# Between the two expert layers of an attention kernel: a row operation ahead of list bookkeeping, two weight loads put behind the last scatter, and weight splits ahead of the transposes

## The chip, the cores and the metric

The program runs on one core of a Trainium2 chip. The time is the device time of one execution in microseconds (us); lower is better. The engines are TensorE (PE in the rows; its weight loads are PEld), VectorE (DVE), ScalarE (ACT), GpSimd (POOL) and SyncE (SP, which only issues transfers here). Transfers run on 16 DMA engines. SP's transfers come from the hardware queue, q1 in the rows; GpSimd's indirect gathers and scatters come from the software queue, q0.

## The reference

Attention with a local window and a few global keys gives `x` (3072 rows of 512). Two layers of experts follow, each row going to one of 8 experts:

```python
x = _moe_ref(x=x, **moe_kwargs)       # layer 1: every row with x @ w_skip > 0 goes to its best expert
return _moe2_ref(x=x, **moe2_kwargs)  # layer 2: experts with a fixed capacity

# layer 2
cap = N // E                          # 384 rows for each expert
logits = x @ w_gate
for idx in np.argsort(-logits.flatten()):   # best (row, expert) pairs first
    tok, e = int(idx) // E, int(idx) % E
    if assigned[tok] >= 0 or counts[e] >= cap:
        continue
    assigned[tok] = e
    counts[e] += 1
for e in range(E):
    mask = assigned == e
    h = np.maximum(x[mask] @ w1[e], 0.0)
    out[mask] = h @ w2[e]
```

Layer 2 needs the finished rows of layer 1, both for its logits and as the input of its experts.

## The kernel before

The kernel is written as streams of work that one planner, a clock of estimated engine times that is kept while the program is built (`Clock`, `ck`), puts into one fixed order for each engine. What is said below of the order is settled at build time.

**Experts.** A unit is one expert's list of rows: up to 208 in layer 1 (blocks of 128 and 80), 384 in layer 2 (three blocks of 128). For a unit, the rows are gathered by an indirect transfer (`gather`, tiles `xg`), turned on TensorE (`pt` or `py` <- `ident,xg`), and kept as a high part `xh` (ScalarE) and a low part `xl` (VectorE). Every weight is split in the same way: `wr` is a loaded part (512 KB; there are eight parts to an expert, four of w1 and four of w2), `wh` its high part (ScalarE), `wl` the rest (`wr` - `wh`), on GpSimd in four pieces or on VectorE in one. `mm1` does 12 products into `ph` for each 128 hidden columns (`xh·wh`, `xl·wh`, `xh·wl`, four of each), then `mm2` 9 into `py`.

**Weights.** The class `Weights` keeps the list of parts (`order`), how many are loaded (`loaded`) and split (`split`). There are four `wr` buffers. `preload` issues loads on SP until four are ahead of the splits; `pump` calls `preload` and then splits a part when its moment has come; `need` splits until a part is there. `on_pool` names the parts whose low half GpSimd makes.

**Routing.** Layer 2's assignment is done in eight phases by the stream of kind `main`. A phase finds one expert's threshold in seven steps over the bits of the logits. A step of phases 0 and 1 is: `gm` (VectorE compares), 24 small matmuls `pr<-oh,gm` that count, `fl` (VectorE), one matmul `pr<-fl,wt`, `v_` and two or three small VectorE operations. After the steps come the bookkeeping (`go`, `part`, `PEN`, `AC`, `rem`, `ML`) and the list of rows (`slots`: `ttb`, `tb_rhs`, `fx`, `mp`, `ix`, `ids`). Phase p's `ids` is what unit p of layer 2 gathers by.

**The place of the change.** `hook` is called ahead of each product and lets a waiting stream put its next step first, if its operands are ready by the planner's clock. At the end of layer 1 `mm2_block` does the last expert's products block by block; after the second block (80 rows) `row_late` makes the rows `o` on VectorE and scatters them into `x2d` on GpSimd. Phase 0 of the routing runs beside these products. Then layer 2 starts: `split_next` makes weight splits of its first expert, `units2[0].load()` gathers its rows (from `x2d`, so after the last scatter has landed), `wait_for` runs the streams and lets TensorE do filler products (`warm`: `ph<-ones,tri`) while it waits, and `run_units` starts the products.

```python
            W_.pump()                      # mm2_block, end of each of the eight steps f
        ...
        W_.add((lambda r0, n: w21r[bass.ds(ereg * Dm + r0, n)], ...))   # phase: this expert's parts
        W_.preload()                       # four loads, as soon as the expert is known
        ...
    split_next()
    units2[0].load()
    split_next()
    split_next()
    wait_for(lambda: units2[0].tb == NH, True)   # gathers, transposes, xh and xl of the three blocks
    split_next()
```

Of the kernel before, what the change touches and what calls it, by code (L numbers as in the profile page):

```python
# [163 lines left out]
def tile_attn_moe_moe(ctx: ExitStack, tc: tile.TileContext, q, k, v, n_global, n_local,  # L164
                      w_skip, w_gate, w1, w2, w2_gate, w21, w22, out):
    nc = Chip(tc.nc)
# [9 lines left out]
    E, _, F = w1.shape  # L176
    KC = Dm // 128
    FC = F // 128
# [6 lines left out]
    HI = -(-SLOTS // 128)  # L185
# [256 lines left out]
    class Weights:  # L442
# [29 lines left out]
            t = max(ck.at["pool"], ck.at["pe"] + T_W) + (4 - j) * 2.3  # L472
            return u == self.done + 1 and j < 4 and t > ck.at["pe"] + (FC - self.f) * 4.2 + T_H

        def preload(self):
            while self.loaded < len(self.order) and self.loaded < self.split + 4:
                self.do_load(self.loaded)

        def pump(self, wait=False):

# [4 lines left out]
                        and (self.pools or (u == 0 and j < 4))):  # L485
                    self.do_split(self.order[self.split])

        def do_load(self, i):
            c = self.order[i]
            u, j = divmod(c, NCH)  # L490
            t = wraw.tile([128, 1024], F32, name="wr")
            a = self.src[u][0 if j < 4 else 1]
            if j < 4:
                nc.sync.dma_start(t, a(j * 128, 128))
            else:
                nc.sync.dma_start(t.rearrange("p (c d) -> p c d", c=2),
                                  a((j - 4) * 256, 256).rearrange("(c p) d -> p c d", p=128))
            self.raw[c] = t
            self.loaded += 1
# [38 lines left out]
    W_ = Weights()  # L538
# [152 lines left out]
    def scatter(dst, ids, src, others):  # L691
        nc.gpsimd.memset(spacer, 0.0)
        st = nc.gpsimd.indirect_dma_start(out=dst, out_offset=bass.IndirectOffsetOnAxis(ap=ids, axis=0),
                                          in_=src, in_offset=None, bounds_check=N - 1, oob_is_err=False)
        for o in others:
            tc.declare_no_dep(st.ins, o.ins, reason="rows of other tokens")
        others.append(st)
# [124 lines left out]
    for g in range(-3, NU + 1):  # L822
# [16 lines left out]
        m, t = divmod(g + 4, NG)  # L839
# [35 lines left out]
    class Unit:  # L875
        at, tb, py, defer, xh, x2, turns, third, banks = None, 0, 0, None, None, None, False, False, None
# [203 lines left out]
    def mm1(U_, f, n_tok):  # L1080
        ph = fps.tile([128, 512], F32, name="ph", bufs=2)
        xx = (U_.xh, U_.xl)
        i = 0
        for (a, b_) in P3:
            for c in range(KC):
                hook(W_.parts[U_.g * NCH + c][a], xx[b_][:, c, :n_tok])
                nc.tensor.matmul(ph[:, :n_tok], W_.parts[U_.g * NCH + c][a][:, f * 128:(f + 1) * 128],
                                 xx[b_][:, c, :n_tok], start=i == 0, stop=i == 3 * KC - 1)
                i += 1
        if U_.defer is None:  # L1090
            h2 = ff.tile([128, 2, wide_h], F32R, name="h2", bufs=h2_bufs)
            hh, hl = h2[:, 0], h2[:, 1]
        else:
            hh, hl = U_.h[0][:, f], U_.h[1][:, f]
            if f == FC // 2 and not U_.defer:
                wait_for(lambda: X_.turned == 2)
        nc.scalar.activation(hh[:, :n_tok], ph[:, :n_tok], AF.Relu)

        def low():
            nc.vector.scalar_tensor_tensor(hl[:, :n_tok], ph[:, :n_tok], 0.0, hh[:, :n_tok].bitcast(F32),  # L1100
                                           op0=OP.max, op1=OP.subtract)

        return (hh, hl) if U_.defer is not None else (hh, hl, h2), low
# [20 lines left out]
    def mm2(U_, f, h, nb, low):  # L1124
        if f == 0:
            U_.y = [fps.tile([128, Dm], F32, name=f"py{(tb + U_.py) % 3}") for tb in range(nb)]
        ww = W_.parts[U_.g * NCH + 4 + f // 2]
        o = (f % 2) * Dm
        for tb in range(nb):
            for i, (a, b_) in enumerate(P3):  # L1130
                hook(h[a], ww[b_])
                n = U_.n[tb]
                nc.tensor.matmul(U_.y[tb][:n], h[a][:, tb * 128:tb * 128 + n], ww[b_][:, o:o + Dm],
                                 start=f == 0 and i == 0, stop=f == FC - 1 and i == 2)
            if tb == 0 and low:
                low()
        W_.free = 4 * U_.g + (f + 1) // 2
# [25 lines left out]
    def need(chunk):  # L1163
        while chunk not in W_.parts:
            b4 = W_.split
            W_.pump(True)
            assert W_.split > b4
# [23 lines left out]
            return max(t, ck.at["dve"] - T_SP) if eng == "dve" else t  # L1191

    streams = []

    def order():
        return sorted((s_ for s_ in streams if not s_.busy), key=lambda s_: s_.rank())

    def hook(*aps):

        while streams:  # L1200
            t = max(ck.at["pe"] + T_EPS, ck.ready("pe", (), aps))
            for s_ in order():
                if s_.when() <= t:
                    s_.step()
                    break
            else:
                return

    def warm(until):

        if ck.at["pe"] + 0.11 <= until:
            p = fps.tile([128, 512], F32, name="ph", bufs=2)
            while ck.at["pe"] + 0.11 <= until:
                nc.tensor.matmul(p[:, :256].rearrange("p (a n) -> p a n", a=2), tri, wide_one, start=True, stop=True)

    def wait_for(over, fill=False):
        while not over():
            t = min(s_.when() for s_ in order()) + T_F
            s_ = next(s_ for s_ in order() if s_.when() <= t)
            if unit_no[0] < 0 and s_.kind == "main":  # L1220
                first_ = min((o for o in order() if o.kind != "main"), key=lambda o: o.when(), default=None)
                if first_ and first_.when() < s_.when() + T_M:
                    s_ = first_
            if fill and s_.need[0] != "dve":
                warm(s_.when() - T_U)
            s_.step()
# [106 lines left out]
    def row_late(U_, tb, on_dve=False):  # L1333
        n = ROWS[tb]
        x2 = ff.tile([128, Dm], F32, name=f"o{tb}", bufs=1)[:n]
        if on_dve:
            nc.vector.scalar_tensor_tensor(x2, U_.y[tb][:n], U_.gw[:n, tb:tb + 1], U_.xs[tb][:n, :Dm],
                                           op0=OP.mult, op1=OP.add)
        else:
            nc.scalar.activation(x2, U_.y[tb][:n], AF.Copy, scale=U_.gw[:n, tb:tb + 1])  # L1340
            nc.gpsimd.tensor_tensor(x2, x2, U_.xs[tb][:n, :Dm], op=OP.add)
        scatter(x2d, U_.sid[:n, tb:tb + 1], x2, x2_st)

    def mm2_block(U_, tb):
        n = ROWS[tb]
        y = U_.y[tb] = fps.tile([128, Dm], F32, name=f"py{(tb + U_.py) % 3}")
        for f in range(FC):
            need(U_.g * NCH + 4 + f // 2)
            ww = W_.parts[U_.g * NCH + 4 + f // 2]
            o = (f % 2) * Dm  # L1350
            for i, (a, b_) in enumerate(P3):
                hook(U_.h[a][:, f], ww[b_])
                nc.tensor.matmul(y[:n], U_.h[a][:, f, tb * 128:tb * 128 + n], ww[b_][:, o:o + Dm],
                                 start=f == 0 and i == 0, stop=f == FC - 1 and i == 2)
            if tb == HI - 1:
                W_.free = 4 * U_.g + (f + 1) // 2
            W_.pump()
# [319 lines left out]
    def phase(ph_):  # L1677
# [104 lines left out]
        dv.tensor_scalar(ei, fx[:, 0:1], -1.0, float(E), op0=OP.mult, op1=OP.add)  # L1782
        ereg = nc.sync.value_load(ei[0:1, 0:1], min_val=0, max_val=E - 1)
        W_.add((lambda r0, n: w21r[bass.ds(ereg * Dm + r0, n)], lambda r0, n: w22r[bass.ds(ereg * F + r0, n)]))
        W_.preload()
        if last:
            yield "dve", ()
            dv.tensor_scalar(fe_p, PEN, 0.0, None, op0=OP.is_ge)
# [70 lines left out]
    def routing():  # L1859
        yield from table_rows(units1[E - 1])  # L1860
        for p in range(E):
            yield from phase(p)
# [25 lines left out]
    for U_ in units1[NE:]:  # L1888
        U_.py = 2 * U_.defer
        if U_.g == E:  # L1890
            U_.y = {}
            for tb in range(HI):
                mm2_block(U_, tb)
                row_late(U_, tb, tb == HI - 1)
            continue
        for f in range(FC):
            need(U_.g * NCH + 4 + f // 2)
            mm2(U_, f, [t[:, f] for t in U_.h], HI, None)
            W_.pump()
        for tb in range(HI):  # L1900
            row_late(U_, tb)
# [2 lines left out]
    ff = ctx.enter_context(tc.tile_pool(name="ff", bufs=2))  # L1904
    width = wide_h = CAP
    h2_bufs = LASTF + 1
    W_.on_pool = (2, 3)
    out_st = []

    def put(U_, tb, o):  # L1910
# [45 lines left out]
    def split_next():  # L1956
        need(W_.order[W_.split])
# [3 lines left out]
    units2[0].banks = ("pt", "py1", "py2")  # L1961
    units2[0].load()
    ck.late = 2.0
    split_next()
    split_next()
    wait_for(lambda: units2[0].tb == NH, True)
    split_next()
    warm(ck.ready("pe", (), [units2[0].xh]) - T_U)
    W_.on_pool = range(NCH)

# [35 lines left out]
```

## Time and profile before

| | us |
|---|---|
| median of 3 runs | 784.69 (783.55 to 793.27) |
| the profiled execution | 787.59 |
| its span, first to last instruction | 785.8 |
| TensorE busy in it | 752.7 (96%) |
| VectorE busy | 529.5 (67%) |
| ScalarE busy | 403.0 (51%) |
| GpSimd busy | 463.2 (59%) |

The profiled execution took 1.8 us more than its span, and 2.9 us more than the median of the runs. Times in the rows are counted from the span's start: attention lies ahead of 234 us, layer 1 runs from there to 457 us, layer 2 from 476 us to the end. Busy time of TensorE includes the filler products.

### The profile page before, as it was taken

What the parts mean: (1) busy time and instruction counts of PE and PEld (TensorE: products, weight loads), DVE (VectorE), ACT (ScalarE), POOL (GpSimd) and SP (SyncE); (2) the same over time, 40 slices, a digit from 0 to 9 for tenths busy, and PEclk for the clock granted to TensorE, in tenths of its full rate; (3) what the DMA queues carried; (4) which work ended last, traced back from release to release, by engine and by line L of the source; (5) the groups of instructions that cost most, each with busy time, mean ns of one, the idle gap of its engine ahead of it and who ended that gap; (6) DMA issues with size and microseconds to landing.
All of it is one profiled execution on the core that took longest, in us unless ns stands there. A gap on an engine that the chain in (4) does not pass through costs nothing.

```text
span 785.8 us, 17475 instructions
## 1 busy us (share of the span) xinstructions
PE 752.7 (96%) x5942; PEld 635.8 (81%) x5942; DVE 529.5 (67%) x1950; ACT 403.0 (51%) x934; POOL 463.2 (59%) x807
## 2 busy tenths in 40 slices
PE   6999999899889899999989989999999999999997
PEld 5887777777669899999888667888788888798986
DVE  5987988979456766676763586878778778822110
ACT  4887787887546455465652214344343434445221
POOL 3664556754214556557652636787685959599711
PEclk9999999999999999999999999999999999999999
DMA  8686988987616757677670061636263535455210
GB/s 190 161 215 167 248 225 205 242 213 213 201 28 209 246 186 218 227 234 231 213 245 6 19 219 59 202 102 220 97 201 141 179 135 162 147 176 188 79 41 40
DMA packets 143834, 132.23 MB, mean 168 GB/s; under 512 B 65427, under 2 KB 110739, under 8 KB 143744
## 3 DMA queue, kind: packets, MB, share of 16 engines
q1 hardware_dynamic: 135360, 111.19, 48.3%
q0 software_dynamic: 6784, 19.51, 7.2%
q8 instruction: 48, 0.79, 0.4%
q10 hardware_dynamic: 1600, 0.39, 0.2%
q14 instruction: 42, 0.34, 0.1%
HBM read 108.80 MB, written 22.79 MB: 167 GB/s over the span
## 4 chain that ended last, share of the span: by engine, by line
PE 51%; issue 6%; POOL 5%; DVE 4%; DMA 3%; ACT 1%; POOLq 0%; ACTq 0%; DVEq 0%
PE ph L125 23%; PE py L125 22%; PE pr L125 3%; POOL wl L125 3%; PE pt L125 2%; DMA wr<-in_moe_w_dram 2%; DVE wl L125 1%; ACT wh L125 1%; POOL out_dram L125 1%; DMA xg<-x2d,ids 1%; DVE py L125 0%; POOL x2d L125 0%; POOL xt L125 0%; DVE xl L125 0%; DVE o L125 0%
## 5 line engine op out<-in xcount | busy, mean ns | idle before, releaser
L125 POOL TENSOR_TENSOR wl<-wr,wh 128x256 fp32r<-128x256 f32 x340 | 245.7, 755 | 67.0 <-ACT wh L125 66.5
L125 ACT ACTIVATE wh<-wr 128x1024 fp32r<-128x1024 f32 (+1 forms) x148 | 142.0, 985 | 42.1 <-DMA wr<-in_moe_w_dram 22.2
L125 PE MATMUL py<-wh,h 128*128 128x512 f32 (+1 forms) x448 | 158.1, 405 | 0.0
L125 ACT ACTIVATE h<-ph 128x208 fp32r<-128x208 f32 (+2 forms) x132 | 54.5, 415 | 188.9 <-PE ph L125 184.1
L125 POOL TENSOR_SCALAR pb<-pb,st 128x232 f32<-128x232 f32 (+1 forms) x192 | 83.6, 454 | 73.8 <-ACT pb L125 26.3
L125 DVE SCALAR_TENSOR_TENSOR h<-ph,h 128x208 fp32r<-128x208 f32 (+1 forms) x128 | 58.9, 461 | 98.5 <-ACT h L125 98.3
L125 ACT ACTIVATE pb<-sb,st 128x232 f32<-128x232 f32 (+1 forms) x192 | 113.8, 663 | 10.4 <-DVE st L125 9.9
L125 PE MATMUL ph<-xh,wh 128*128 128x208 f32 (+1 forms) x512 | 100.5, 313 | 1.8 <-DVE h L125 1.8
L125 PE MATMUL ph<-xh,wl 128*128 128x208 f32 (+1 forms) x512 | 101.1, 313 | 0.0
L125 PE MATMUL ph<-xl,wh 128*128 128x208 f32 (+1 forms) x512 | 99.4, 313 | 0.0
L125 PEld LDWEIGHTS py<-wh,h 128*128 128x128 f32 (+1 forms) x448 | 81.7, 186 | 14.3
L125 PE MATMUL py<-wl,h 128*128 128x512 f32 (+1 forms) x224 | 90.3, 403 | 0.0
L125 PEld LDWEIGHTS ph<-xh,wh 128*128 128x128 f32 x512 | 83.2, 192 | 7.1 <-DVE h L125 1.9
L125 PEld LDWEIGHTS ph<-xl,wh 128*128 128x128 f32 x512 | 80.0, 193 | 1.4 <-issue 1.0
L125 PEld LDWEIGHTS ph<-xh,wl 128*128 128x128 f32 x512 | 80.2, 193 | 0.2
L125 DVE TENSOR_TENSOR wl<-wr,wh 128x1024 fp32r<-128x1024 f32 x51 | 66.0, 1300 | 18.5 <-ACT wh L125 17.2
L125 DVE CUSTOM_DVE_ANT_0 sb<-pS,bias 128x232 f32<-128x232 f32 (+1 forms) x192 | 61.4, 375 | 8.6 <-PE pS L125 7.2
L125 DVE COPY pts<-pP 116x512 f32<-116x512 f32 (+1 forms) x96 | 60.7, 672 | 7.6 <-PE pP L125 7.1
L125 PE MATMUL pS<-kt,qt 64*128 64x232 f32 (+1 forms) x384 | 50.6, 382 | 1.0 <-ACT pb L125 1.0
L125 POOL DMA_INDIRECT xg<-x2d,ids x24 | 23.2, 968 | 47.6 <-DVE py L125 31.4
L125 PE MATMUL pP<-ident,pb 128*116 128x128 f32 (+1 forms) x384 | 50.7, 275 | 0.0
L125 PE MATMUL pO<-pts,vw 116*64 116x128 f32 x640 | 46.3, 281 | 4.0 <-DVE pts L125 2.6
(461 smaller groups left out, 1276.3 us busy)
## 6 DMA issues: line engine op xcount, KB each, us to landing
wr<-in_moe_w_dram SPq DMA_DIRECT2D x136, 512.0 KB
xd<-xs SPq DMA_DIRECT2D x32, 192.0 KB
x2d<-xs SPq DMA_DIRECT2D x32, 192.0 KB
kraw<-in_k_dram SPq DMA_DIRECT2D x30, 192.0 KB
qraw<-in_q_dram SPq DMA_DIRECT2D x30, 192.0 KB
vw<-in_v_dram SPq DMA_DIRECT2D x32, 160.0 KB
vw<-in_v_dram SPq DMA_DIRECT2D x32, 120.0 KB
xT<-in_moe_w_dram SPq DMA_DIRECT2D x1, 1536.0 KB
```

Source lines behind the costliest of these rows:

```text
L125: r = f(*a, **k)
```

## The change

The edits:

- **A hold on the routing.** From the seventh of the eight steps of the last expert's second block on, `hook` no longer lets the stream `main` put steps that start on VectorE ahead of the products. The hold ends after `row_late`.
- **Two loads instead of four.** Phase 0 preloads two weight parts instead of four. After the hold ends, `preload(4, True)` loads up to four, and writes one element of each buffer on GpSimd ahead of the load (`gate`).
- **One more split on VectorE.** Of the first four parts of layer 2, GpSimd makes the low half of one (number 3) instead of two (2 and 3).
- **Splits ahead of the transposes.** The fourth `split_next` moves ahead of `wait_for`.

```diff
-        def preload(self):
-            while self.loaded < len(self.order) and self.loaded < self.split + 4:
-                self.do_load(self.loaded)
+        def preload(self, ahead=4, gate=False):
+            while self.loaded < len(self.order) and self.loaded < self.split + ahead:
+                self.do_load(self.loaded, gate)
...
+            if gate:
+                nc.gpsimd.memset(t[0:1, 0:1], 0.0)
...
-                if s_.when() <= t:
+                if s_.when() <= t and not (held_back and s_.kind in held_back and s_.need[0] == "dve"):
...
+            if tb == HI - 1 and f == FC - 2:
+                held_back.append("main")
...
-        W_.preload()
+        W_.preload(4 if ph_ else 2)
...
+            held_back.clear()
+            if len(W_.order) > W_.split:
+                W_.preload(4, True)
             continue
...
-    W_.on_pool = (2, 3)
+    W_.on_pool = (3,)
...
-    split_next()
-    split_next()
+    for _ in range(3):
+        split_next()
     wait_for(lambda: units2[0].tb == NH, True)
-    split_next()
```

**VectorE, from the last two list operations ahead of the last expert's rows.** `o` is the row operation; `go`, `part`, `PEN` and `AC` are bookkeeping. Before:

```order
L125 CAST tb_rhs<-py_7053 128x24
L125 TENSOR_TENSOR go<-oh,py_7053 128x192
L125 TENSOR_TENSOR py_7053<-py_7053,fe 128x24
L125 TENSOR_REDUCE part<-go 128x8
L125 TENSOR_TENSOR py_7053<-py_7053,code 128x24
L125 SCALAR_TENSOR_TENSOR PEN<-py_7053,PEN 128x24
L125 TENSOR_TENSOR AC<-AC,py_7053 128x24
L125 SCALAR_TENSOR_TENSOR o_7549<-py_7405,gwt,xg_6495 80x512
L125 COPY fx<-pt 128x1
```

And now:

```order
L125 CAST tb_rhs<-py_7053 128x24
L125 SCALAR_TENSOR_TENSOR o_7541<-py_7405,gwt,xg_6495 80x512
L125 COPY fx<-pt 128x1
L125 TENSOR_TENSOR fx<-fx,py_7053 128x1
L125 TENSOR_SCALAR tb_rhs<-fx 128x1
L125 TENSOR_SCALAR pt<-islot,fx 128x384
L125 TENSOR_TENSOR tb_rhs<-pt,tb_rhs 128x1
L125 SCALAR_TENSOR_TENSOR mp<-islot,fx,pt 128x384
L125 TENSOR_TENSOR go<-oh,py_7053 128x192
```

The row operation and six list operations now stand ahead of six bookkeeping operations. Later on VectorE three splits `wl` follow `ids`, where two did, and `rem` and `ML` stand behind them.

**GpSimd, from the scatter of the last expert's first block.** `x2d<-o` are the scatters, `xg<-x2d` the gathers of layer 2's first expert. In the changed program:

```order
L125 DMA x2d<-o_7398,sid 3072x512
L125 MEMSET spacer 1x1
L125 DMA x2d<-o_7541,sid 3072x512
L125 DMA xg_7604<-x2d,ids 128x512
L125 DMA xg_7606<-x2d,ids 128x512
L125 DMA xg_7608<-x2d,ids 128x512
L125 TENSOR_TENSOR wl<-wr,wh 128x256 x20
```

No write into a `wr` buffer stands between the last scatter and the gathers, nor anywhere else: `pump` at the end of the same step of `mm2_block` has called `preload` with its default of four, so that nothing is left for the gated call. On SP the order of all transfers is the same as before; the four loads of w1 stand behind the read of the expert's number (`ei`) in both:

```order
L120 TENSOR_LOAD ei
L120 ISA x2
L125 ISA
L125 DMA wr<-in_moe_w_dram 128x1024
L125 ISA
L125 DMA wr<-in_moe_w_dram 128x1024
L125 ISA
L125 DMA wr<-in_moe_w_dram 128x1024
L125 ISA
L125 DMA wr<-in_moe_w_dram 128x1024
```

**ScalarE, behind the last rows of layer 1.** `wh` are high parts of weights, `xh` those of the gathered rows. Before:

```order
L125 ACTIVATE wh<-wr 128x1024 x3
L125 ACTIVATE xh<-pt 128x4x128
L125 ACTIVATE xh<-py_7772 128x4x128
L125 ACTIVATE xh<-py_7818 128x4x128
L125 ACTIVATE wh<-wr 128x1024
L125 ACTIVATE h_7961<-ph 128x384
```

And now:

```order
L125 ACTIVATE wh<-wr 128x1024 x4
L125 ACTIVATE xh<-pt 128x4x128
L125 ACTIVATE xh<-py_7751 128x4x128
L125 ACTIVATE xh<-py_7769 128x4x128
L125 ACTIVATE h_7852<-ph 128x384
```

All four high parts are now made ahead of the first `xh`. On TensorE, counted in the order between the last product of layer 1 and the first of layer 2: 72 counting matmuls (three routing steps) before, 24 (one step) now; the other two steps now stand among the products of layer 2's first expert. The fillers there are 106 before and 104 now, 66 of them in one row ahead of the first gathered block now. In the whole program two splits move from GpSimd to VectorE (340 pieces before, 332 now).

## Rows read from the trace of the kernel before

**Rows 1.** Busy time by engine, clock, DMA share in stretches: PE, PEld, DVE, ACT, POOL.

```profile
520.00:560.00 40.00, 40.00 (x253) 32.67 (x251) 31.03 (x136) 15.89 (x24) 32.13 (x48) 1.00 0.43 145
```

**Rows 2.** Timeline of TensorE between the layers: start, us, operation, idle before.

```profile
462.78 4.86 PE L125 MATMUL ph<-ones,tri 128*128 128x256 bf16 x43
...
470.72 0.66 PE L125 MATMUL pt<-ident,xg 128*128 128x128 f32 x4 [1.50 <-DMA xg<-x2d,ids]
...
476.20 0.76 PE L125 MATMUL ph<-xh,wh 128*128 128x384 f32 x3
...
478.38 0.44 PE L125 MATMUL ph<-xl,wh 128*128 128x384 f32 x1
```

**Rows 3.** Timeline of GpSimd: the last scatter and the first gather.

```profile
459.72 0.92 POOL L125 DMA_INDIRECT x2d<-o,sid  x1 [6.82 <-DVE fx L125]
...
466.21 1.00 POOL L125 DMA_INDIRECT xg<-x2d,ids  x1 [5.57 <-DVE py L125]
```

**Rows 4.** Timeline of VectorE from the last product of layer 1.

```profile
457.33 0.17 DVE L125 CAST tb_rhs<-py 128x24 bf16<-128x24 f32 x1
...
458.70 0.74 DVE L125 SCALAR_TENSOR_TENSOR o<-py,gwt,xg 80x512 f32<-80x512 f32 x1
...
462.45 0.16 DVE L125 SCALAR_TENSOR_TENSOR ids<-pt,ix 128x3 int32<-128x3 f32 x1
462.53 1.23 DVE L125 TENSOR_TENSOR wl<-wr,wh 128x1024 fp32r<-128x1024 f32 x1
```

**Rows 5.** DMA queues, 460.7 to 463.0 us: packets, MB, share of 16 engines.

```profile
q1 hardware_dynamic: 220, 0.79, 96.2%
```

**Rows 6.** DMA queues, 463.0 to 465.5 us.

```profile
q1 hardware_dynamic: 109, 0.32, 52.4%
q0 software_dynamic: 64, 0.15, 15.1%
```

**Rows 7.** DMA issues, 444.4 to 446.0 us: the scatter issued there, us to landing.

```profile
x2d<-o,sid POOLq DMA_INDIRECT x1, 2.4
```

**Rows 8.** DMA queues and issues, 383.1 to 386.0 us, in layer 1.

```profile
q1 hardware_dynamic: 303, 1.11, 97.9%
...
xg<-xd,gid POOLq DMA_INDIRECT x1, 5.6
```

**Rows 9.** Timeline of SP: weight loads.

```profile
456.44 2.16 SPq L125 DMA_DIRECT2D wr<-in_moe_w_dram  x4
...
472.58 0.37 SPq L125 DMA_DIRECT2D wr<-in_moe_w_dram  x1
```

**Rows 10.** DMA queues, 467.2 to 468.9 us.

```profile
q1 hardware_dynamic: 219, 0.44, 68.0%
q0 software_dynamic: 1, 0.00, 0.6%
```

**Rows 11.** Chain that ended last, two routing steps beside products in layer 1.

```profile
446.36 0.69 PE pr L125 x24
...
447.81 1.59 PE py L125 x6
449.40 0.69 PE pr L125 x24
```

**Rows 12.** Stretches again: the last products, and the start of layer 1.

```profile
776.00:780.00 4.00, 4.00 (x19) 3.26 (x18) 0.00 (x0) 0.60 (x1) 2.10 (x4) 1.00 0.16 66
234.00:238.00 4.00, 3.92 (x22) 3.46 (x23) 2.01 (x3) 2.87 (x4) 1.70 (x2) 0.57 0.39 110
```

**Rows 13.** Timeline of TensorE at the start of layer 1.

```profile
234.08 1.54 PE L125 MATMUL py<-ident,xg 128*128 128x128 f32 x8 [2.14 <-issue]
```

**Rows 14.** Timeline of GpSimd and TensorE: the second expert's third block.

```profile
501.08 0.95 POOL L125 DMA_INDIRECT xg<-x2d,ids  x1 [0.30 <-issue]
...
513.39 0.60 PE L125 MATMUL pt<-ident,xg 128*128 128x128 f32 x4
```

More of the change, by code (lines that the diff above doesn't have):

```diff
@@ L486, in pump, with do_load @@
                     self.do_split(self.order[self.split])
-        def do_load(self, i):
+        def do_load(self, i, gate=False):
             c = self.order[i]
@@ L1193, in tile_attn_moe_moe @@
     streams = []
+    held_back = []
     def order():
```

## The prediction

> **What bounds the kernel now.** I read the stretches first. From the second expert of layer 2 on TensorE is busy all the time: 40.00 of 40.00 us between 520 and 560 [rows 1]. So whatever moves the first product of layer 2, at 476.20 us [rows 2], moves the end by as much, and whatever is added to TensorE behind it is paid in full. The change touches the road to that product, so I read the timeline there, engine by engine. The reader is to see three things.
>
> First, TensorE has nothing but fillers to do, and at the end nothing at all: it sits idle for 1.50 us until the first gathered block lands at 470.7 [rows 2]. Second, the gather starts only at 466.21, though its list `ids` is ready at 462.6 [rows 3, 4]: it waits for the last scatter, issued at 459.72, to land. Third, the queues say why that takes so long. From 460.7 to 463.0 us all packets are of the hardware queue, the four weight loads issued at 456.44 to 458.60; the scatter's 64 packets move from 463.0 on, when those loads run out [rows 5, 6, 9]. The same scatter without loads beside it lands 2.4 us after its issue [rows 7], here the wait is 6.5 us. In layer 1 a gather issued in the middle of loads fares alike: its queue shows no packet in 383.1 to 386.0, and it lands after 5.6 us [rows 8].
>
> **The change part by part.** The sum is made against the profiled execution (787.59 us), in differences, and laid on the median of the runs, 784.69.
>
> *The row operation first.* The last list operation ahead of it begins at 457.33, so `o` can begin at about 457.5 instead of 458.70 [rows 4]: 1.2 us earlier, and the scatter with it, at 458.5. What is late next is the queue: the fourth load is still issued by 458.60 [rows 9], so the scatter still stands behind all four, whose packets run out at the same time. I take no gain, since the case of rows 8 (issued among the loads, drained behind them) is the nearest; the bounds are 0 and -1.2.
>
> The Trainium skill has another rule: its page "DMA: Bandwidth & Descriptors", section "Queues, rings and completion order", says that each DMA engine takes turns between the queues that have work. By that rule the scatter would not wait for the loads to drain, and the 1.2 us would be had in full. The trace speaks against it: 220 packets of one queue and none of the other in 2.3 us, with the scatter's issue done [rows 3, 5].
>
> *Two loads behind the scatter.* The order shows that this does not happen: the four loads stand in SP's queue as they did, with no write of GpSimd ahead of them. Cost and gain 0, both bounds: the operations are not in the program.
>
> *Bookkeeping behind the list.* `ids` comes about 0.5 us sooner (1.2 for `o` and the six operations moved up, less the 1.3 of bookkeeping, plus the 0.6 of `rem` and `ML`, which move behind it). That list was ready 3.6 us before the gather began [rows 3, 4], so it is worth nothing.
>
> *The third split on VectorE.* It gives its `wr` buffer back when the three splits, one of 1.23 us each [rows 4], are through, at 465.6 to 466.1. GpSimd's version came behind the three gathers and freed it at 472.58, when SP issues that load [rows 9]. So a 512 KB load moves from behind the gathers to right ahead of them. Before, the gathers' packets wait for the one load that runs at 467.2 to 468.9 (219 packets to 1) [rows 10]; now two follow each other. A load needs 1.5 us at 0.79 MB in 2.3 us [rows 5]. The bounds are 0 and +1.5; I take half, **+0.7**, since the load in front is moved up by 0.5 and part of the second falls into the 0.5 us that the gathers need to start anyway (an estimate from the middle of the bounds). The first block lands at 471.4.
>
> *From the landing to the first product.* Before: 470.72 to 476.20, 5.5 us, with two more routing steps put in between. Now the order has 12 transposes (3 times 0.6 to 0.66), 24 counting matmuls (0.69), one `fl` matmul and 15 fillers of 0.113 (4.86 us for 43) [rows 2, 11], 4.5 us in all. VectorE's `xl` and `fl` and ScalarE's `xh` end within that. **-1.0**. Moving the fourth high part ahead of the transposes lies under the wait for the gather and costs nothing: its load has drained by 464 [rows 6].
>
> *Waits among the first products.* Before, three products of 0.18 each from 476.20, one step's count of 0.69 and one more product should end at 477.6; the next starts at 478.38 [rows 2, 11]. These 0.8 us were waits for that step's `gm` and for the last `xl`. Now the fillers stand where the first was, and the third `xl` comes a step earlier against the products. **-0.8**, bounds 0 and -0.8.
>
> *Two routing steps more among the products.* Before, three steps are counted in the time that TensorE waits anyway; now one. All seven phases have to be done, so two steps go to where TensorE is full. What a step costs there: in layer 1 a step and eight products take 3.04 us; at 0.265 a product (1.59 for six) a step is 0.9, at 0.21 (19 in 4.00 us) it is 1.36 [rows 11, 12]. I take 1.15: **+2.3**, bounds +1.8 and +2.7.
>
> *The clock.* Fillers now end before the gather lands: 66 of them at 0.113 from about 460.9 last until 468.3, and then TensorE idles for 2.4 us (landing at 470.7) to 3.1 us (471.4), where it idled for 1.50. At the start of layer 1 it idled for 2.14 us, and behind that the granted clock was 0.57 on the average of 234 to 238 us, so at the lower of the two levels, 1.2 GHz, for most of it [rows 12, 13]; that cost (1 - 0.57) times 4.0, 1.7 us. After the 1.50 us the clock stayed at 2.4 GHz. The longer idle is nearest to the 2.14 us, so I count on a fall. The bounds are 0 and +1.7; part of the slow time may pass while TensorE still waits, so I take **+1.2**.
>
> The sum: 0 + 0.7 - 1.0 - 0.8 + 2.3 + 1.2 = +2.4 us. That makes 787.1 for the median, and a span of 788.2 in a profile like the one before. This is 0.3% slower, well inside the 2% (15.7 us) that a measurement of this kernel can tell from no change.
>
> **The rivals.** *The clock holds.* For it: the fall depends on more than the length of the idle time, and the rows have one case either way. Then +1.2, **785.9**.
>
> *The queues share.* If the scatter, 1.2 us earlier, also lands 1.2 us earlier, the gathers start at 465.0, ahead of the third load; the first block lands near 469.5, the idle time is 1.2 us and the clock holds: -1.2 - 1.0 - 0.8 + 2.3 = -0.7, **784.0**. Against it speak rows 5, 6, 8 and 10. This is where the page's turn-taking would lead.
>
> *The steps are free.* If gaps of TensorE among the first expert's products swallow the two counts, 2.3 us fall away: **784.8**. Against it: TensorE shows no free time beside routing [rows 1].
>
> *The list comes late.* This ends on the slower side. The routing of phase 1 runs two steps later against the products, 3.04 us each at the pace of rows 11, so 6 us. The second expert's third block is gathered from 501.08 (landed some 3.3 us later) and turned at 513.39 [rows 14], a slack of 9 us. If other work delays the stream by three more steps, the lag is 15 us, TensorE waits for 6, and the time is **793**. It decides at a lag of 9 us.
>
> *The change does what it says.* With two loads less ahead of it the scatter would land up to 3 us sooner; the order excludes it.
>
> **How the numbers follow.** Forecast 0.45, clock holds 0.22, queues share 0.17, steps free 0.08, late list 0.05, others 0.03. The range goes from the case of shared queues, less the 1.1 us by which the fastest run lies under the median, 783.0, to the forecast with the upper bounds of load, steps and clock (+0.8 + 0.4 + 0.5, so 788.8) and some of the same spread, 789.5. That leaves out the late list and some of the edges. No case reaches 2% on either side; faster by 2% has 0.01, slower by 2% 0.02 (a late list that repeats in later phases), within 0.97.
>
> **What the profile would show.** The scatter issued near 458.5 but the gathers still beginning near 466 say that the queue decides; a gather at 465.0 or before says that they share. A weight load issued near 466 and a first gathered block after 471 confirm the collision. The clock column between 470 and 476 shows whether it fell. The first product near 476 to 477, and 150 counting matmuls in the first expert instead of 108, show that the gain went into the two steps. A first product before 474 with the end unmoved would still fit the steps; an end moved with it would break that term. The prediction is wrong if the scatter lands early, or if the planner's new order of the later experts differs by more than a microsecond or two.

## The result and the profile after

The changed kernel takes 790.36 us (median of 13 runs, 788.85 to 794.68) where the kernel before takes 786.64 in the runs beside it (13 runs, 783.02 to 793.27). The ratio is 1.0057, with an interval of 1.0041 to 1.0073, so 3.2 to 5.7 us slower. The forecast was 2.4 us slower, 787.1; the direction holds, the time is outside the range. A part of that is the base: the forecast was laid on a median of three runs, 784.69, and the 13 runs of the same kernel here have 786.64.

The two profiled executions ran apart by 3.9 us ahead of the transition already: the `ttb` matmul right behind the last product of layer 1 starts at 457.47 before and at 453.54 after. So all times of the road below are counted from that matmul. TensorE (start, us, operation, idle before), first that matmul in the kernel before, then the changed kernel:

```profile
457.47 0.16 PE L125 MATMUL pt<-ttb,tri 128*128 128x1 bf16 x1
```

```profile
453.54 0.16 PE L125 MATMUL pt<-ttb,tri 128*128 128x1 bf16 x1
...
456.92 7.37 PE L125 MATMUL ph<-ones,tri 128*128 128x256 bf16 x66
467.94 1.09 PE L125 MATMUL pt<-ident,xg 128*128 128x128 f32 x4 [3.66 <-DMA xg<-x2d,ids]
...
474.51 0.95 PE L125 MATMUL ph<-xh,wh 128*128 128x384 f32 x4
...
517.29 0.97 PE L125 MATMUL ph<-xh,wh 128*128 128x384 f32 x4 [0.69 <-ACT xh L125]
...
519.13 0.44 PE L125 MATMUL ph<-xl,wh 128*128 128x384 f32 x1 [0.50 <-DVE xl L125]
```

Against [rows 2] the reader is to see three things: the fillers end early and TensorE idles for 3.66 us instead of 1.50; the first product comes 20.97 us behind `ttb` (474.51 - 453.54) where it came 18.73 behind it; and there are two waits of 1.2 us together at the first products of the *second* expert. The clock, in the stretches behind that idle time (last three columns: granted clock, DMA share, GB/s):

```profile
466.00:467.00 1.00, 0.00 (x0) 0.00 (x0) 0.00 (x0) 0.00 (x0) 1.00 (x2) 0.96 1.07 430
467.00:473.00 6.00, 5.06 (x42) 3.75 (x43) 1.76 (x5) 1.57 (x3) 1.00 (x2) 0.50 0.54 167
473.00:474.00 1.00, 1.00 (x8) 0.75 (x6) 0.93 (x5) 0.22 (x1) 0.00 (x0) 0.63 0.00 0
```

So 1.2 GHz for over six microseconds, in which the transposes, counts and last fillers run at half speed. GpSimd shows scatter and gather, to be laid beside [rows 3]:

```profile
454.65 0.91 POOL L125 DMA_INDIRECT x2d<-o,sid  x1 [5.69 <-DVE fx L125]
461.68 1.00 POOL L125 DMA_INDIRECT xg<-x2d,ids  x1 [6.12 <-DVE wl L125]
```

The scatter is issued 1.11 us behind `ttb` instead of 2.25, as forecast, and the gather begins at 8.14 instead of 8.74. The queues, first from the scatter's issue to 458.4, then from the first gather's issue to 465.5:

```profile
q1 hardware_dynamic: 310, 1.11, 102.8%
```

```profile
q1 hardware_dynamic: 566, 1.09, 93.8%
```

No packet of the software queue moves in either stretch, as in [rows 5] (in [rows 10] it is one): scatter and gathers wait until the weight loads run out. And the 24 row outputs of layer 2 on ScalarE (first and last start), in the kernel before and in the changed one:

```profile
L125 ACT ACTIVATE o<-py x24: 597/597/600, 520.1 to 780.8; 128x512 f32<-128x512 f32 x24
```

```profile
L125 ACT ACTIVATE o<-py x24: 597/597/600, 521.7 to 782.8; 128x512 f32<-128x512 f32 x24
```

From the first product to the first of them 43.9 us pass before and 47.2 now; from there to the last one 260.7 before and 261.1 now. So in these two traces the changed kernel lost 2.2 us on the road to the first product and 3.7 us behind it.

### The profile page after: what moved, and what is told of

Read it like the earlier page. It is cut to its first block, busy times and chain, and to the rows that moved or that the text cites. A ratio compares the mean times of both kernels' runs of the same rounds, so it can differ in the third digit from the quotient of the medians.

```text
span 787.8 us, 17463 instructions
## 1 busy us (share of the span) xinstructions
PE 753.7 (96%) x5940; PEld 635.1 (81%) x5940; DVE 529.4 (67%) x1952; ACT 403.3 (51%) x934; POOL 454.9 (58%) x799
## 4 chain that ended last, share of the span: by engine, by line
PE 50%; POOL 6%; issue 6%; DVE 4%; DMA 2%; ACT 1%; POOLq 0%; SPq 0%; DVEq 0%; ACTq 0%
PE ph L125 23%; PE py L125 21%; POOL wl L125 5%; PE pr L125 4%; PE pt L125 2%; DVE wl L125 2%; DMA wr<-in_moe_w_dram 1%; ACT wh L125 1%; POOL out_dram L125 1%; DMA xg<-x2d,ids 1%; DVE py L125 0%; DVE xl L125 0%; DVE h L125 0%; POOL xg L125 0%; DVE gm L125 0%
## 5 line engine op out<-in xcount | busy, mean ns | idle before, releaser
L125 POOL TENSOR_TENSOR wl<-wr,wh 128x256 fp32r<-128x256 f32 x332 | 237.9, 749 | 72.9 <-ACT wh L125 72.5
L125 PEld LDWEIGHTS py<-wh,h 128*128 128x128 f32 (+1 forms) x448 | 81.8, 186 | 14.2
L125 DVE TENSOR_TENSOR wl<-wr,wh 128x1024 fp32r<-128x1024 f32 x53 | 67.6, 1282 | 19.3 <-ACT wh L125 19.3
L125 PE MATMUL py<-h,wh 128*128 128x416 f32 x192 | 47.6, 361 | 2.8 <-DVE h L125 2.8
```

The costliest lines, as they stand in the source:

```text
L125: r = f(*a, **k)
```

## The experiments

All kernels at once. Columns: routing steps counted ahead of the first product; then, in us from `ttb`, the first gather's begin, the first transposes, the first product; the way from first product to first row output; from there to the last; the sum; the time against the kernel before on the same chip (ratio times 786) with its interval.

```
kernel            steps gather turned first  rest1  rest2   sum   time against before
before              3    8.74  13.25  18.73  43.9  260.7  323.3
before, again (e12) 3   10.76  14.23  21.02  43.8  260.8  325.7
changed             1    8.14  14.40  20.97  47.2  261.1  329.3  +4.5 [+3.2, +5.7]
changed, again (e10)1    8.98  13.57  20.26  47.2  261.1  328.5  +3.9 [+1.7, +6.0]
e1 more fillers     1    8.47  14.28  18.54  47.4  261.1  327.0  +3.5 [+1.4, +5.4]
e2 fewer fillers    3    8.13  12.86  21.03  43.9  260.7  325.6  +2.3 [+0.2, +4.4]
e3 hold alone       2    7.91  12.20  18.60  45.0  261.2  324.8  +0.6 [-1.3, +2.5]
e4 gate at work     1    5.06  10.82  16.56  47.1  261.1  324.8  +3.5 [+1.4, +5.7]
e5 splits alone     2   10.34  13.98  21.53  44.8  261.3  327.7  -0.5 [-2.4, +1.5]
e6 2 on GpSimd      2    8.34  12.22  17.50  44.8  261.6  323.9  -0.6 [-2.7, +1.5]
e7 gate, 3 steps    3    4.98  11.16  18.01  43.9  260.7  322.6  -1.8 [-3.9, +0.3]
e8 gathers first    2    5.07   9.50  15.96  44.8  261.2  322.0  -3.1 [-4.9, -1.2]
e9 seventh load     1    8.74  13.11  20.18  47.2  261.0  328.4  +3.0 [+0.5, +5.5]
e11 one split       2    5.07   9.29  16.63  44.9  261.3  322.8  -2.7 [-5.0, -0.3]
```

The two columns "rest" repeat to 0.4 us in all kernels with the same number of steps; the road ahead of them does not, not even for one and the same kernel. Against the mean of the two traces of before (324.5) the sums agree with the measured times within 1.3 us, but for e4 and e5. The times go by the number of steps more than by the road: kernels with one step lie at +3.0 to +4.5, although their roads run from 16.56 to 20.97 us; those with two lie at -3.1 to +0.6, those with three at -1.8 to +2.3.

**e1, the clock.** 34 more fillers at the end of the row of 66, the planner's clock set back behind them:

```diff
+            at = ck.at["pe"]
+            for _ in range(more.pop() if more else 0):
+                nc.tensor.matmul(p[:, :256]..., tri, wide_one, start=True, stop=True)
+            ck.at["pe"] = at
...
+    more[:] = [34, 0]
     wait_for(lambda: units2[0].tb == NH, True)
```

> The changed kernel with 34 more filler products (0.11 us each) ahead of the first gathered block's transposes, nothing else moved. In the changed kernel TensorE idles for 3.66 us there, the granted clock is 0.50 from 467 to 473.5 us, and 6.57 us pass from the landing to the first product. Theory 'the clock': the idle time goes, the clock stays at 1.00, the way from landing to first product shrinks to the 4.5 us of its operations, and the time falls by 2.1 us against the changed kernel (from +4.5 to about +2.4 us against the kernel before). Rival 'the order': VectorE's xl and the one routing step set that way, the clock hides behind them: change below 0.5 us.

```profile
466.00:475.00 9.00, 9.00 (x98) 7.76 (x96) 4.69 (x15) 1.79 (x3) 4.66 (x6) 1.00 0.67 238
```

TensorE is busy for all nine microseconds, the clock stays at 2.4 GHz, and from the turning of the first block to the first product 4.26 us pass instead of 6.57 (6.69 in the changed kernel's other trace, e10): the clock cost 2.3 us in the first trace of the changed kernel. The time falls by 1.0 us at the middle of the intervals, less than 2.1; these overlap.

**e2, the idle time alone.** 33 of the 58 fillers of [rows 2]'s wait left out of the kernel before:

```diff
+                skip -= 1
+                if skip >= 0:
+                    ck.at["pe"] += 256 / 2400.0
+                    continue
...
+    fewer.append(33)
```

> The kernel before with 33 of its 58 filler products in a row left out, so that TensorE idles for about 3.7 us ahead of the first routing step's counts; nothing else is moved. Theory 'the clock': the idle time alone brings the granted clock down to 0.50 for the transposes that follow, and the time rises by 1 to 2 us. Rival 'the idle time is harmless': the clock holds, or falls only while TensorE waits anyway, and the change is below 0.4 us.

```profile
466.29 0.79 PE L125 MATMUL pr<-oh,gm 128*32 128x8 bf16 x24 [3.56 <-DVE gm L125]
```

```profile
466.00:467.00 1.00, 0.71 (x24) 0.70 (x24) 0.56 (x2) 0.00 (x0) 0.69 (x2) 0.68 0.58 186
467.00:476.00 9.00, 8.46 (x70) 5.69 (x68) 5.13 (x17) 2.74 (x4) 3.68 (x6) 0.50 0.54 182
```

After 3.56 us of idle time the clock falls and stays at 1.2 GHz for nine microseconds, though TensorE is busy for 8.46 of them. The first block comes early (12.86), and yet the first product is 2.3 us later than in the first trace of before: from the turning to it 8.17 us pass instead of 5.48. The time (+2.3, from +0.2 to +4.4) fits the theory of the clock, at the upper end of its price. The place of the first product alone would not show it, since the second trace of before (e12), without this edit, has it at 21.02 too.

**e3, the hold alone,** put into the kernel before; loads and splits stay as they were:

```diff
+                if s_.when() <= t and not (held_back and s_.kind in held_back and s_.need[0] == "dve"):
...
+            if tb == HI - 1 and f == FC - 2:
+                held_back.append("main")
...
+            held_back.clear()
             continue
```

> The kernel before with the hold alone: the row operation 1.2 us earlier, four loads, GpSimd's two splits and the fourth split as before. The planner now puts two routing steps instead of three ahead of the first product, and 62 fillers in one row. Theory 'queue, steps and clock': the gather starts at most 0.6 us earlier, one step more stands among the products (+1.2), TensorE idles for 2 to 3 us ahead of the first block and the clock falls (+1.5): +2 to +3 us against the kernel before. Rival 'the hold pays': the scatter lands 1.2 us earlier, and with it everything: -1 to 0 us.

The first block is turned at 12.20, 1.0 and 2.0 us sooner than in the two traces of before, but only 0.7 sooner than in e2, which has no hold either; so the hold probably pays more than I gave it. The step costs what it was said to (1.1 and 0.5), and the time is +0.6 us. The clock fell here as well, late and for about three microseconds (0.50 in 470 to 472 us). Neither theory had it whole: the sum lies between them.

**e4, the gate at work.** A limit that `preload` and `pump` both obey:

```diff
-            while self.loaded < len(self.order) and self.loaded < self.split + ahead:
+            while self.loaded < len(self.order) and self.loaded < self.split + min(ahead, self.limit):
...
-        W_.preload(4 if ph_ else 2)
+        W_.limit = 4 if ph_ else 2
+        W_.preload()
...
+            W_.limit = 4
             W_.preload(4, True)
```

> The changed kernel with its gate at work: a limit of two loads holds until the last row operation is done, so that two loads really stand behind the last scatter, each behind a one-element write of GpSimd. Theory 'the drain decides': with two loads less ahead of it the scatter lands some 2 us sooner, the first gathered block too, TensorE idles for less than 2 us, the clock holds, and the time falls by 3 to 4 us against the changed kernel, to between 0 and +1.5 us against the kernel before. Rival 'the loads hold it anyway': the two gated loads, issued while the scatter's packets still wait, keep it back as before, or the third split on VectorE waits for its late load and delays the routing: no gain against the changed kernel, +4 to +6 us against the kernel before.

```profile
456.73 0.91 POOL L125 DMA_INDIRECT x2d<-o,sid  x1 [5.67 <-DVE fx L125]
457.64 0.12 POOL L125 MEMSET wr<- 1x1 f32 x2
460.68 1.62 POOL L125 DMA_INDIRECT xg<-x2d,ids  x1 [2.93 <-DVE ids L125]
```

With two loads ahead of it the scatter's 64 packets are through 3.2 us after its issue, and the gather begins 3.1 us sooner than in the changed kernel; now the list `ids` releases it and no transfer. The drain of the queue is what held it. In this trace the first product is 4.4 us sooner. The time, however, misses the theory's 0 to +1.5: it is only about 1 us under the changed kernel's, where the trace's sum says 4. The profiled execution was 2 us faster than the median of this kernel's runs, which may be part of it; the rest of the difference stays open.

**e5, the two split edits alone** in the kernel before:

```diff
-    W_.on_pool = (2, 3)
+    W_.on_pool = (3,)
...
-    split_next()
-    split_next()
+    for _ in range(3):
+        split_next()
     wait_for(lambda: units2[0].tb == NH, True)
-    split_next()
```

> The kernel before with the two split edits alone (the third split on VectorE, the fourth split ahead of the transposes), without the hold and with the preload as it was. Two routing steps stand ahead of the first product instead of three, 69 fillers in one row. From the hold run: a step moved among the products costs 1.1 us and the planner's later order 0.5 us. Theory 'the load in front of the gathers': the third split on VectorE lets one load more run ahead of the gathers, the first block lands 0.7 to 1.5 us later than before, TensorE idles for some 2 us and the clock falls: +3 to +5 us against the kernel before. Rival 'the split is free': first product as before, +1.6 us.

In the trace the theory's picture stands: gather at 10.34, an idle time of 2.12 us, clock at 0.50, first product at 21.53. But the time shows none of it (-0.5 us), and the mean granted clock of its 12 runs is 0.993 where the profiled one had 0.988. So the trace is no guide to this kernel's time. The time is: in the kernel before, the two split edits cost at most 1.5 us, and the theory's +3 to +5 is out.

**e6, two splits on GpSimd again** in the changed kernel:

```diff
-    W_.on_pool = (3,)
+    W_.on_pool = (2, 3)
```

> The changed kernel with two of the first four splits on GpSimd again, as before the change; hold and order of the splits stay. Two steps ahead of the first product, 62 fillers and 16 counts ahead of the first gathered block. Theory 'the third split on VectorE was the costly edit': this run comes out like the hold alone (first product within 0.3 us of the kernel before, +1.1 for one step, +0.5 later), +0.5 to +2 us against the kernel before, 2.5 to 4 us under the changed kernel. Rival 'the fourth split ahead costs': it comes out within 1 us of the changed kernel.

It comes out like the hold alone (-0.6 and +0.6 us, first block at 12.22 and 12.20): the fourth split ahead of the transposes costs nothing, and in the changed kernel the third split on VectorE, with what the planner makes of it, was the costly edit. By itself it isn't: e5 has it at -0.5 us. The hold alone makes +0.6, the split edits alone -0.5, both together +4.5: each alone takes out one of the three steps ahead of the first product, both together take out two. Undoing it brings back one of the two lost steps, lets the first block come over a microsecond sooner, and the 1.2 us of waits at the second expert are gone.

**e7 and e8, combinations.** e7 is e4 with the splits as before the change (the edits of e5 undone) and another allowance of the planner for the gather:

```diff
-    ck.late = 1.7
+    ck.late = 2.2
```

e8 is e4 with e6's edit, `ck.late` at -0.3, and a bound in `preload` (`min(..., self.cap)`) that holds the fifth load until the gathers are issued:

```diff
+        W_.cap = 1000 if ph_ else W_.split + 4
...
     units2[0].load()
+    W_.cap = 1000
+    W_.preload(4, True)
```

> A combination: the hold, the gate at work (two loads behind the last scatter), two splits on GpSimd and the fourth split behind the transposes as before, and the planner's allowance for the gather at 2.2 us instead of 1.7, so that three routing steps stand ahead of the first product and everything from there on is in the order of the kernel before. Theory: the gather lands 2.4 us earlier as in the gate run, no step is added among the products, TensorE does not idle long and the clock holds; VectorE's steps then set the first product at about 17.5 us behind the last product of layer 1 instead of 18.7: -1 to -1.5 us against the kernel before. Rival 'late weights': the parts that are loaded behind the scatter are split too late for the first product: 0 to +2 us.

> A combination that goes further: the hold, the gate at work, two splits on GpSimd, the fourth split ahead of the transposes, and the fifth load held by a one-element write that stands behind the third gather on GpSimd, so that no weight load runs between the scatter and the gathers but the two gated ones; the planner's allowance for the gather is -0.3 us. Two steps stand ahead of the first product. Theory 'loads ahead of the gathers hold them': the first block lands some 4 us sooner than in the kernel before, the first product comes 2.5 to 3.5 us sooner, one step more costs 1.1 and the later order 0.5: -1 to -2 us against the kernel before. Rival 'late w2': the parts of w2, loaded 3 us later, make the first expert's second products wait: 0 to +2 us.

e8's queues, first from the first gather's issue to 464.5 us, while the two gated loads run, then from there to 466.5 us:

```profile
q1 hardware_dynamic: 168, 0.57, 74.3%
q8 instruction: 1, 0.02, 3.1%
```

```profile
q0 software_dynamic: 88, 0.29, 58.6%
q1 hardware_dynamic: 5, 0.01, 1.5%
```

e7 comes out at -1.8 us, in its theory's direction, with an interval that reaches +0.3. In e8 the first gather still waits for the two gated loads, and then the three run with hardly a load beside them: the first block is turned at 9.50 and the first product comes at 15.96, as its theory said; no wait shows up for the parts of w2. e8 is faster than the kernel before (ratio 0.9961, interval 0.9938 to 0.9985), by somewhat more than forecast. The gate alone does not do this: the change with its gate at work is e4, at +3.5.

**e9, the seventh load held** behind the third gather, with e8's bound in `preload`, all else as changed:

```diff
+        W_.cap = 1000 if ph_ else W_.split + 6
...
-    for _ in range(3):
-        split_next()
+    split_next()
+    W_.preload()
+    split_next()
+    W_.cap = 1000
+    W_.preload(4, True)
+    split_next()
```

> The changed kernel with one load held back: the third weight load behind the first four (the seventh of the expert), which the third split on VectorE lets go ahead of the gathers, now waits for a one-element write that stands behind the third gather on GpSimd. Splits, fillers and routing steps stay as in the changed kernel. Theory 'that load is what the third split on VectorE costs': the first block is turned some 12.2 us behind the last product of layer 1 (as with the split on GpSimd) instead of 14.4, TensorE idles for about 1.5 us instead of 3.66, the clock holds, the first product comes 4.4 us sooner than in the changed kernel: +1 to +2 us against the kernel before. Rival 'VectorE itself costs it' or 'the fifth and sixth load hold the gathers': the first block stays beyond 13.5 us and the time at +3 to +5 us.

Neither: the first block comes at 13.11, between 12.2 and 14.4 (13.57 in the changed kernel's other trace), and the clock falls here too. By these three traces the load is worth 0.5 to 1.3 us, near the 0.7 of the forecast; but the changed kernel's two traces differ by 0.8 themselves, so this is not shown. The time, +3.0, is nearer to the rivals', but its interval holds both. The rest of the way from 12.2 to some 14 isn't explained by it, and stays open.

**e10 and e12, both kernels again,** without an edit.

> The changed kernel once more, on the chip of the other runs of this call. If the picture of its first trace holds in other executions (first block at 14.4 us, clock at 0.50 for six to seven us, first product at 21.0 us behind the last product of layer 1), its time is 3 to 5 us over the kernel with the seventh load held, and 4 to 6 us over the kernel before. Rival 'the clock fell in that one execution': the clock holds here and the time is at +2.5 to +3.5 us.

> The kernel before once more, for a second trace of it. If the first trace is typical, the first product comes 18.7 us behind the last product of layer 1 with the clock at 1.00 throughout; if the clock falls there too in some executions, it comes some 2 us later.

The changed kernel repeats its picture (idle 2.84 us, clock at 0.50, first product at 20.26). Its time, +3.9 against the kernel before, is a little under the 4 to 6 that its theory gave, and only 0.8 over e9's, where it gave 3 to 5. But the kernel before does not repeat *its* picture. Its gathers and TensorE:

```profile
458.38 0.91 POOL L125 DMA_INDIRECT x2d<-o,sid  x1 [6.82 <-DVE fx L125]
466.90 1.00 POOL L125 DMA_INDIRECT xg<-x2d,ids  x1 [7.61 <-DVE gm L125]
```

```profile
470.37 1.12 PE L125 MATMUL pt<-ident,xg 128*128 128x128 f32 x4 [2.49 <-DMA xg<-x2d,ids]
...
477.16 0.77 PE L125 MATMUL ph<-xh,wh 128*128 128x384 f32 x3
```

The gather begins at 10.76 instead of 8.74, TensorE idles for 2.49 us, the clock falls (0.50 in 470 to 473 us) and the first product comes at 21.02. What was late is in the queues of 463.2 to 466.9 us: the last four of the scatter's 64 packets move beside 477 of the next loads, the last one between 465.2 and 465.7. In the first trace the last ones moved by 465.0; in both the gather begins 1.2 to 1.7 us later.

```profile
q1 hardware_dynamic: 477, 0.93, 88.5%
q8 instruction: 1, 0.02, 1.7%
q0 software_dynamic: 4, 0.01, 1.0%
```

**e11, one split on VectorE,** put into e8:

```diff
-    W_.on_pool = (2, 3)
+    W_.on_pool = (1, 2, 3)
...
-    ck.late = -0.3
+    ck.late = -1.3
```

> The combination with the gathers first (hold, gate, fifth load behind the third gather), and of the first four splits only one on VectorE, three on GpSimd behind the gathers; the planner's allowance for the gather is -1.3 us. Two routing steps ahead of the first product. Theory 'VectorE's chain of splits, list and steps sets the first product now': with 1.23 us less on it the first product comes 14.7 us behind the last product of layer 1 instead of 16.0: -2 to -3 us against the kernel before. Rival 'GpSimd is late': its three splits of 2.77 us end at 17.3 us, and the first products wait for them: 0 to -1 us.

The first product comes at 16.63, later than in e8 and than the theory's 14.7; the time, -2.7 us, lies where the theory put it, but is no further gain over e8's. Not GpSimd's splits but gaps ahead of the transposes (1.61, 0.34 and 1.06 us) show in its trace; so neither theory's reason is seen.

## Why the prediction was wrong, step by step

**The steps that failed lie behind the first product.** I had -0.8 for waits there and +2.3 for two routing steps, together +1.5; both traces of both kernels give +3.7 (43.9 + 260.7 against 47.2 + 261.1). Three parts. *A step's size:* in the changed kernel 12 products and one step take 3.37 us (474.51 to 477.88), and 12 products at 0.175 take 2.1, so a step costs 1.3 rather than 1.15, within the bounds that I gave.

```profile
475.38 0.76 PE L125 MATMUL pr<-oh,gm 128*32 128x8 bf16 x24
...
477.88 0.34 PE L125 MATMUL ph<-xh,wh 128*128 128x384 f32 x1
```

*The waits:* 0.5 us went (`gm` and `fl`), not 0.8. These are the two in the kernel before:

```profile
477.22 0.76 PE L125 MATMUL pr<-oh,gm 128*32 128x8 bf16 x24 [0.26 <-DVE gm L125]
...
484.85 0.16 PE L125 MATMUL pr<-fl,wt 32*128 32x8 bf16 x1 [0.24 <-DVE fl L125]
```

*The list that comes late:* the sum had nothing for it, and as a rival it was real and mis-sized. I put its slack at 9 us, from the landing of the second expert's third block to its turning [rows 14], and let it decide beyond that. The third gather now begins 30.0 us behind the first product (504.48 - 474.51) instead of 24.9, and already TensorE waits for `xh` and `xl`, 0.69 and 0.50. It does not wait for the gather, which lands some 3.8 us later, so that 7.7 us of slack are left ahead of the turning at 515.97. But the planner has put the third turning 1.3 us ahead of the second expert's first product instead of 3.6, and on VectorE a `gm` of the routing stands ahead of that block's `xl`. First the kernel before, then the changed one, GpSimd, TensorE and VectorE:

```profile
516.98 0.86 PE L125 MATMUL ph<-xh,wh 128*128 128x384 f32 x4
```

```profile
504.48 0.95 POOL L125 DMA_INDIRECT xg<-x2d,ids  x1 [0.30 <-issue]
515.97 0.64 PE L125 MATMUL pt<-ident,xg 128*128 128x128 f32 x4
517.30 0.95 DVE L125 TENSOR_TENSOR gm<-m,py 128x768 bf16<-128x768 f32 x1
518.39 0.68 DVE L125 TENSOR_TENSOR xl<-pt,xh 128x512 fp32r<-128x512 f32 x1
```

That the planner does so because the list is later is likely, but not tested by itself. Steps 2.6, waits 1.2, less 0.5, make 3.3; the remaining 0.4 lies behind the first row output, where I did not look further. e3, e5, e6, e8 and e11, with one step more than before among the products instead of two, pay 1.4 to 1.8 us and none of the waits at the second expert.

**The base.** Of the 3.3 us between the forecast's 787.1 and the measured 790.36, 1.95 are the base: three runs of the kernel before were too few for its median. As a difference, +2.4 stands against +3.7 by the medians and +4.5 by the ratio.

**The clock, right in kind.** It fell, and cost 2.3 us in the first trace (e1), not 1.2 and not within 1.7. But as a term of the *difference* it was wrong for another reason: the kernel before falls too in some of its executions (e12). I took one trace of before, in which the clock held, for the rule. How often it falls is not shown: the clock over a whole execution is 0.992 in both traces of before, with and without the fall. Over the runs its median is 0.992 for the kernel before (29 runs) and 0.991 for the changed one (12) on the chip of e9 to e12, so a part of the difference may well be left.

**The road as a whole.** Forecast +0.9 (load 0.7, way to the first product -1.0, clock 1.2). The first two traces give +2.2; the means of the two traces each, 19.9 and 20.6, give +0.7. With +3.7 behind it that is +4.4, against a measured +4.5 and +3.9. That the forecast of the road comes out so near is in part luck: its terms were off in both directions, and the two traces of one kernel lie 2.3 and 0.7 us apart.

**The row operation first.** Given as 0, bounds 0 and -1.2. The scatter's packets indeed wait for the four loads (310 to 0), whenever it is issued. Yet kernels with the hold and two splits on VectorE turn the first block at 12.2, those without the hold at 12.9 to 14.2. The packets are through sooner once the gap opens, and fewer of them are left for the next loads to delay; this reading rests on e12's four packets and is not tested by itself. By these traces the value was near the lower bound.

**The load in front of the gathers,** +0.7, fits e9 (0.5 to 1.3), as far as one trace goes. **Landing to first product,** -1.0: without the clock it went from 5.48 to 4.26 us (e1), -1.2; in e4, also with one step and the clock up, it is 5.74, since the second block lands later there. **Fourth split ahead and no gate,** both 0: right (e6, and the order).

**Queues that share.** The Trainium skill's turn-taking rule ("DMA: Bandwidth & Descriptors", section "Queues, rings and completion order") would have let the gathers in beside the loads. The traces show no turns packet by packet: while loads fill the queue the gathers move nothing, 566 packets to none in the changed kernel and 168 to none in e8; they run when the loads are through, 88 to 5 in e8. In e4 gathers do get in among later loads, but in long stretches: no packet of theirs in 463.3 to 464.5 us beside 190 of the loads, then this up to 465.7, then 3 beside 120 up to 466.3:

```profile
q0 software_dynamic: 77, 0.26, 53.7%
q1 hardware_dynamic: 131, 0.24, 51.2%
```

## What to carry to other kernels

A single trace of an interleaved transition is one draw: compare two traces of the same kernel before a wait or a clock level is made a term. Where the bottleneck engine waits for a transfer, count what else it could do in that wait; work that a reordering pushes out of it is paid in full later, here some 1.6 us for one routing step and 3.7 for two. Two edits that are harmless alone can be costly together, when each takes work out of the same wait. In these kernels small indirect transfers did best when the bulk loads on the other queue were held until they were through (e8).

## What the runs showed of the hardware

Two things I had not expected. The clock, once down, stayed at 1.2 GHz for over nine microseconds of nearly full work (e2). Idle times of 1.32 us (e6) and 1.39 us (e4) left it at 2.4, and one of 1.30 us (e3) was followed by a fall: their length alone doesn't tell. In this order, e6, e4, e3 and the clock of e3:

```profile
472.78 0.63 PE L125 MATMUL pt<-ident,xg 128*128 128x128 f32 x4 [1.32 <-DMA xg<-x2d,ids]
468.89 0.63 PE L125 MATMUL py<-ident,xg 128*128 128x128 f32 x4 [1.39 <-DMA xg<-x2d,ids]
467.92 0.63 PE L125 MATMUL pt<-ident,xg 128*128 128x128 f32 x4 [1.30 <-DMA xg<-x2d,ids]
470.00:471.00 1.00, 1.00 (x6) 0.88 (x5) 0.90 (x6) 0.34 (x1) 0.00 (x0) 0.50 0.02 8
```

And four left-over packets of a scatter, moving beside the next loads, went with a gather that began 2 us later in one execution of an unchanged kernel.
